# Attention on one core: score and value matmuls in runs of nine pairs instead of three, row sums off TensorE, one FFN unit per half

## Chip, cores, metric

One core of a Trainium2 chip runs the whole program. The metric is device time in microseconds (us) from one launch. The kernel before takes 952.02 us, the median of 3 runs (951.53 to 952.89).

## The reference

Two blocks follow each other, in float32. The first is attention over 8 batches, 8 heads, 1152 keys and head size 64. Its queries are the means of two neighbours, so there are 576 of them.

```python
q_pool = q.reshape(B, H, S // 2, 2, D).mean(axis=3)
scores = (1 / np.sqrt(D)) * np.matmul(q_pool, k.transpose(0, 1, 3, 2))
attn = np.exp(scores - scores.max(-1, keepdims=True))
attn = attn / (attn.sum(-1, keepdims=True) + 1e-09)
x = np.matmul(attn, v)            # then (B, H, S, D) -> (B, S, H*D): 576 rows of 512
```

The second, for each batch, takes the 128 rows of x with the highest gate score and adds an FFN's result to them; other rows pass through.

```python
scores = np.einsum('bsd,d->bs', x, w_gate)
top = np.argpartition(-scores[b], 128)[:128]
h = np.maximum(x[b, top] @ w1, 0.0)             # 512 -> 1024
out[b, top] = x[b, top] + sigmoid(scores[b, top])[:, None] * (h @ w2)
```

## The kernel before

Heads are worked in pairs, 32 pairs in all, four to a batch. A pair's keys lie in 9 chunks of 128, its 576 queries in two halves of 288. The scores of one chunk and one half are two matmuls, one per head, on the upper and the lower 64 rows of TensorE (L710): this is a *score pair*. It writes one PSUM buffer of two banks (pool `ps_sc`, three buffers). ScalarE takes the exponential of both heads in one instruction (L717), without a maximum. The *value pair* of the chunk is again two matmuls, one per head, on the left and the right 64 columns (L727); nine such pairs add up in one PSUM bank `av`. The profile shows each float32 matmul as two instructions, so a pair counts four.

The order of the work is written out in `run` and kept (`manual_schedule`): each engine does its instructions in the order in which they are written. The loop takes steps. A step is a group of three chunks (`G = 3`): three score pairs of this group, then three value pairs of the group before. Three steps are a half, six a pair of heads.

The row sums of the exponentials are made in two parts: `added` (L745, L755, L756) adds the nine chunks of a half on VectorE, and in `normalized` two matmuls with ones (L770) sum over the partitions, a step after the half's end. VectorE turns `av` into the layout of x by 32x32 transposes (`drained`, L760). There is only one `av` buffer, so the next half's first value matmul waits for that. `normalized` also transposes the sums (L778), adds 1e-9 (L780), takes the reciprocal (L784) and multiplies (L786), all on VectorE. Once a pair, `finished` writes x to a scratch tensor in DRAM (SyncE's queue, L798), multiplies by the gate weights on GpSimd (L803) and sums on VectorE (L809).

`load_pair` brings k, q and v of the next pair on SyncE's queue, two buffers each for k and q. `prepare_pair` adds neighbouring queries on GpSimd (L692) and transposes k and q on VectorE (L697, L698), in a pair's fourth step.

`routed` is a generator with the FFN block of one batch: one unit of it is issued in each step that does not normalise. Its parts are the gate's row sums (`line`, `diag`, L826, L830), their spread over all partitions by matmul (L842) and copy on ScalarE (L849), the scores as columns (L651), the gate's exponential on ScalarE (L858), the ranks by comparisons on VectorE (L880 to L910), the picks (L916), their matmul (L926), a gather (L938), the transposes of the picked rows (L953), the FFN's matmuls (L965 in two units, L977), and a scatter (L992). It uses the one PSUM buffer of `misc`. The last batch runs its generator after the loop. `outside` (L1009 to L1025) counts sums out of bounds, for a slower path that isn't taken here.

Of the kernel before, what the change touches and what calls it, by code (L numbers as in the profile page):

```python
# [13 lines left out]
G = 3  # L14
# [520 lines left out]
class _Plain:  # L535
# [10 lines left out]
    def __init__(self, ctx, tc, q, k, v, moe_w_gate, moe_w1, moe_w2, capacity, out):  # L546
# [43 lines left out]
        self.ps_ms = pool("ps_ms", 1, space=psum)  # L590
        self.constants()
# [8 lines left out]
    def constants(self):  # L600
# [29 lines left out]
        self.columns(self.token, line_f)  # L630
# [9 lines left out]
        self.sums = const.tile([P, self.B * self.NPAIR * 2, self.HB], F32, name="sums")  # L640
# [4 lines left out]
    def columns(self, to, line):  # L645

        nc, NF = self.nc, self.NF
        ps = self.misc()
# [19 lines left out]
    def load_pair(self, b, hp):  # L668
        nc = self.nc
        kb = self.load.tile([P, self.KB, BLK], F32, name="kb")  # L670
        qb = self.load.tile([P, self.QB, 2, BLK], F32, name="qb")
        v_sb = self.load.tile([P, 2, self.NC, self.D], F32, name="v_sb", bufs=3)
        for j, ds, rows in self.quarters():
            h = 2 * hp + j
            nc.sync.dma_start(  # L675
                kb[rows, :, :], self.k[b, h, :, ds].rearrange("(n i) d -> i n d", i=BLK)
            )
            nc.sync.dma_start(  # L678
                qb[rows, :, :, :].rearrange("i n r d -> i (n r) d"),
                self.q[b, h, :, ds].rearrange("(i m) d -> i m d", i=BLK),  # L680
            )
# [6 lines left out]
    def prepare_pair(self, pair):  # L688

        nc = self.nc  # L690
        qp = self.load.tile([P, self.QB, BLK], F32, name="qp", bufs=1)
        nc.gpsimd.tensor_tensor(  # L692
            out=qp[:, :, :], in0=pair["q"][:, :, 0, :], in1=pair["q"][:, :, 1, :], op=ALU.add
        )
        pair["kT"] = self.load.tile([P, self.S], F32, name="kT")
        pair["qT"] = self.load.tile([P, self.Sp], F32, name="qT")
        nc.vector.transpose(pair["kT"][:, :], pair["k"].rearrange("p n d -> p (n d)"))  # L697
        nc.vector.transpose(pair["qT"][:, :], qp.rearrange("p n d -> p (n d)"))  # L698

    def scores(self, grp):  # L700

        nc, pair, n = self.nc, grp["pair"], self.HALF
        qs = slice(grp["s"] * n, (grp["s"] + 1) * n)
        grp["p"] = self.work.tile([P, G, 2, n], F32, name="p", bufs=5)
        for u in range(G):
            c = grp["g"] * G + u
# [10 lines left out]
            nc.scalar.activation(grp["p"][:, u, :, :], sc[:, :, 0:n], AF.Exp, scale=self.scale)  # L717

    def weighted(self, grp):

        nc, n = self.nc, self.HALF
        if grp["g"] == 0:
# [425 lines left out]
```

## Time and profile before

| | us |
|---|---|
| median of 3 runs | 952.02 |
| the profiled execution | 951.33 |
| its span (first to last instruction) | 949.5 |
| TensorE matmuls busy | 844.1 (89%) |
| VectorE busy | 629.0 (66%) |
| ScalarE busy | 359.5 (38%) |
| GpSimd busy | 109.4 (12%) |
| mean granted clock of TensorE, of full | 0.946 |

The rest of the profiled execution's time lies around the span. Busy times overlap. A matmul's end is modelled, so a high share of TensorE does not by itself say that it runs at its best; what it does in a stretch is read from the starts of its runs. An instruction waits for a semaphore at the head of its engine's queue, and what is behind it waits too. [...]

### The profile page before, as it was taken

How to read it: one execution, taken by the hardware profiler on the slowest of the kernel's cores; microseconds unless marked ns; L12 is line 12 of the kernel's file. 1: busy time of each engine (PE TensorE's matmuls, PEld its weight loads, DVE VectorE, ACT ScalarE, POOL GpSimd, SP SyncE). 2: the span in 40 equal slices, each digit the busy share in tenths (PEclk: the TensorE clock that was granted, in tenths of full speed). 3: DMA queues.
4: the chain of work that ended last, by engine and by line, in shares of the span. 5: the costliest groups of instructions: out<-in, count | busy, mean ns of one | idle time of the engine just before them, and what ended most of it. 6: DMA issues, size and time to landing. Idle time of an engine off the chain costs nothing.

```text
span 949.5 us, 14253 instructions
## 1 busy us (share of the span) xinstructions
PE 844.1 (89%) x5695; PEld 500.2 (53%) x5695; DVE 629.0 (66%) x1069; ACT 359.5 (38%) x625; POOL 109.4 (12%) x91
## 2 busy tenths in 40 slices
PE   4999888998899988999879989799889998889736
PEld 2555545654456554565446545465455654556324
DVE  2888777566875678746787376865777567874540
ACT  2544443434343344325424344343443334433200
POOL 1111111011110111102011111011111011110100
PEclk9999998999999999999999999899998999989958
DMA  9987774766834676545767437557464667810120
GB/s 134 249 135 103 125 105 60 83 99 109 104 56 61 94 138 88 76 61 74 125 88 99 60 77 117 82 88 99 89 97 64 76 99 118 108 24 7 25 67 14
DMA packets 453419, 84.97 MB, mean 89 GB/s; under 512 B 450528, under 2 KB 450528, under 8 KB 453088
## 3 DMA queue, kind: packets, MB, share of 16 engines
q1 hardware_dynamic: 452064, 79.79, 57.5%
q0 software_dynamic: 1280, 4.20, 1.6%
q8 instruction: 46, 0.75, 0.4%
q14 instruction: 29, 0.24, 0.1%
HBM read 72.42 MB, written 20.97 MB: 98 GB/s over the span
## 4 chain that ended last, share of the span: by engine, by line
issue 39%; PE 27%; DVE 18%; SPq 5%; POOL 5%; DMA 4%; ACT 2%; POOLq 0%; DVEq 0%
PE sc L710 9%; PE av L727 8%; DVE acc L745 6%; PE ps L965 6%; DMA qb<-in_q_dram 3%; POOL qp L692 3%; SPq L675 2%; SPq L798 2%; DVE cmp L889 2%; PE ps L977 1%; SPq L678 1%; ACT p L717 1%; DVE sum L755 1%; POOL prod L803 1%; PE ps L926 1%
## 5 line engine op out<-in xcount | busy, mean ns | idle before, releaser
L717 ACT ACTIVATE p<-sc 128x576 f32<-128x576 f32 x576 | 336.1, 651 | 408.3 <-PE sc L710 389.6
L710 PE MATMUL sc<-qT,kT 64*128 64x288 f32 x2304 | 352.3, 438 | 9.9 <-DVE qT L698 9.9
L727 PE MATMUL av<-p,v_sb 128*64 128x288 f32 x2304 | 332.2, 425 | 22.7 <-DVE avb L760 22.7
L710 PEld LDWEIGHTS sc<-qT,kT 64*128 64x128 f32 x2304 | 221.0, 195 | 124.3 <-issue 71.8
L727 PEld LDWEIGHTS av<-p,v_sb 128*64 128x64 f32 x2304 | 152.3, 140 | 181.7 <-issue 77.1
L745 DVE TENSOR_TENSOR acc<-p 128x1728 f32<-128x1728 f32 x64 | 124.6, 1947 | 115.4 <-ACT p L717 115.1
L745 DVE TENSOR_TENSOR acc<-acc,p 128x1728 f32<-128x1728 f32 x64 | 137.0, 2141 | 10.0 <-ACT p L717 9.5
L803 POOL TENSOR_TENSOR prod<-x,w_gate 128x576 f32<-128x576 f32 x32 | 44.9, 1403 | 568.9 <-DVE x L786 568.9
L760 DVE STREAM_TRANSPOSE avb<-av 128x288 f32<-128x288 f32 x64 | 30.6, 478 | 60.0 <-PE av L727 60.0
L965 PE MATMUL ps<-xeT,w 128*128 128x128 f32 x512 | 63.4, 284 | 1.4 <-ACT hT L972 0.7
L965 PEld LDWEIGHTS ps<-xeT,w 128*128 128x128 f32 x512 | 60.3, 197 | 8.1 <-issue 5.3
L977 PE MATMUL ps<-w,hT 128*128 128x512 f32 x128 | 57.1, 599 | 0.7 <-ACT hT L972 0.7
L809 DVE TENSOR_REDUCE part<-prod 128x18 f32<-128x576 f32 x32 | 24.1, 753 | 48.7 <-POOL prod L803 48.7
L755 DVE TENSOR_TENSOR sum<-acc 128x576 f32<-128x576 f32 x64 | 49.6, 775 | 2.2
L756 DVE TENSOR_TENSOR sum<-sum,acc 128x576 f32<-128x576 f32 x64 | 49.6, 775 | 2.2
L692 POOL TENSOR_TENSOR qp<-qb 128x576 f32<-128x576 f32 x32 | 45.9, 1435 | 22.8 <-DMA qb<-in_q_dram 22.6
L697 DVE STREAM_TRANSPOSE kT<-kb 128x1152 f32<-128x1152 f32 x32 | 43.0, 1345 | 6.2 <-DMA kb<-in_k_dram 6.2
L770 PE MATMUL ps<-sum,ones 128*64 128x288 f32 x256 | 42.7, 413 | 1.5 <-DVE sum L756 1.5
L977 PEld LDWEIGHTS ps<-w,hT 128*128 128x128 f32 x128 | 23.7, 190 | 30.7 <-issue 29.8
L926 PE MATMUL ps<-meta,pick 128*128 128x3 f32 (+1 forms) x80 | 15.3, 310 | 27.3 <-DVE pick L916 27.3
L972 ACT ACTIVATE hT<-ps 128x512 f32<-128x512 f32 x16 | 9.6, 597 | 73.8 <-PE ps L965 73.8
L984 DVE SCALAR_TENSOR_TENSOR xe<-ps,own_gate,xe 128x512 f32<-128x512 f32 x8 | 6.0, 751 | 41.9 <-PE ps L977 41.9
(64 smaller groups left out, 307.6 us busy)
## 6 DMA issues: line engine op xcount, KB each, us to landing
kb<-in_k_dram SPq DMA_DIRECT2D x128, 144.0 KB, 4.6
qb<-in_q_dram SPq DMA_DIRECT2D x128, 144.0 KB, 4.8
v_sb<-in_v_dram SPq DMA_DIRECT2D x64, 288.0 KB, 5.3
xs<-x SPq DMA_DIRECT2D x128, 72.0 KB, 2.3
out_dram<-xs SPq DMA_DIRECT2D x8, 1152.0 KB, 5.7
w<-in_moe_w_dram SPq DMA_DIRECT2D x2, 2048.0 KB, 11.1
xe<-xs,index POOLq DMA_INDIRECT x8, 3.5
out_dram<-xe,index POOLq DMA_INDIRECT x8, 4.4
```

The costliest lines, as they stand in the source:

```text
L692: nc.gpsimd.tensor_tensor(out=qp[:, :, :], in0=pair["q"][:, :, 0, :], in1=pair["q"][:, :, 1, :], op=ALU.add)
L697: nc.vector.transpose(pair["kT"][:, :], pair["k"].rearrange("p n d -> p (n d)"))
L710: nc.tensor.matmul(sc[:, j, 0:n], lhsT=pair["kT"][rows, c * P : (c + 1) * P], rhs=pair["qT"][rows, qs], start=True, stop=True,)
L717: nc.scalar.activation(grp["p"][:, u, :, :], sc[:, :, 0:n], AF.Exp, scale=self.scale)
L727: nc.tensor.matmul(self.av[j * self.D : (j + 1) * self.D, 0:n], lhsT=grp["pair"]["v"][:, j, c, :], rhs=grp["p"][:, u, j, :], start=(c == 0 ...
L745: nc.vector.tensor_tensor(out=acc[:, :, :], in0=first[:, :, :], in1=grp["p"].rearrange("p u j n -> p u (j n)"), op=ALU.add,)
L755: nc.vector.tensor_tensor(out=to, in0=acc[:, 0, :], in1=acc[:, 1, :], op=ALU.add)
L756: nc.vector.tensor_tensor(out=to, in0=to, in1=acc[:, 2, :], op=ALU.add)
L770: nc.tensor.matmul(ps[j * self.D : (j + 1) * self.D, 0:n], lhsT=self.ones[:, 0 : self.D], rhs=half["sum"][:, j, :], start=True, stop=True,)
L803: nc.gpsimd.tensor_tensor(out=prod[:, :, :], in0=x[:, hp, :, :], in1=self.w_gate[:, hp : hp + 1, :].broadcast_to([P, self.QB, BLK]), op=AL ...
L965: nc.tensor.matmul(pv[:, f, 0:w], lhsT=self.w1[:, c, (f0 + f) * P : (f0 + f + 1) * P], rhs=xeT[:, c, 0:w], start=(c == 0), stop=(c == self ...
L977: nc.tensor.matmul(ps[0:w, 0 : self.Dm], lhsT=hT[:, f, 0:w], rhs=self.w2[:, f, :], start=(f == 0), stop=(f == self.NFC - 1),)
```

## The change

- `scores` and `weighted` work a whole half: nine score pairs of half h, then nine value pairs of half h - 1. The exponentials of a half are one tile.
- The row sums are made by `folded`: GpSimd adds chunks 0 to 2 and 3 to 5; VectorE sums that and chunks 6 to 8 with two reduces that transpose 32x32 blocks on the way (so they sum over 32 partitions), and a third small reduce. One matmul a pair with a 0/1 matrix (`merge`) sums over the four blocks of partitions and spreads the result.
- `normalized` works once a pair. The product of `avb` and the reciprocals moves from VectorE to GpSimd.
- FFN units are issued at one point of each half, after the value pairs (`between`), one unit of each active generator. Those with larger outputs take a buffer of `ps_sc`. L965 becomes one unit; the two row matmuls and their copies become one.
- k and q get one buffer instead of two. The first pair is loaded and prepared in two parts, its q by ScalarE's queue. The weights' loads come one half later; a pair is prepared at the start of the half before it is used.
- After the loop the comparisons are not divided into units, and `outside` runs behind the gather.

```diff
+        self.merge = const.tile([P, P // BLK, BLK], F32, name="merge")
+        nc.vector.tensor_copy(
+            self.merge[:, :, :], self.same[:, :].unsqueeze(1).broadcast_to([P, P // BLK, BLK])
+        )
...
-    def load_pair(self, b, hp):
+    def load_pair(self, b, hp, parts=1):
-        kb = self.load.tile([P, self.KB, BLK], F32, name="kb")
-        qb = self.load.tile([P, self.QB, 2, BLK], F32, name="qb")
+        kb = self.load.tile([P, self.KB, BLK], F32, name="kb", bufs=1)
+        qb = self.load.tile([P, self.QB, 2, BLK], F32, name="qb", bufs=1)
+        nk, nq = self.KB // parts, self.QB // parts
+        other = nc.sync if parts == 1 else nc.scalar
...
-    def scores(self, grp):
+    def scores(self, half):
-        grp["p"] = self.work.tile([P, G, 2, n], F32, name="p", bufs=5)
-        for u in range(G):
-            c = grp["g"] * G + u
+        p = half["p"] = self.work.tile([P, self.NG, G, 2, n], F32, name="p")
+        for c in range(self.NC):
             sc = self.ps_sc.tile([P, 2, 512], F32, name="sc")
...
-            nc.scalar.activation(grp["p"][:, u, :, :], sc[:, :, 0:n], AF.Exp, scale=self.scale)
+            nc.scalar.activation(p[:, c // G, c % G, :, :], sc[:, :, 0:n], AF.Exp, scale=self.scale)
...
+    def folded(self, half):
+        nc, nb, p, pair = self.nc, 2 * self.HB, half["p"], half["pair"]
+        acc = self.work.tile([P, G * 2 * self.HALF], F32, name="acc")
+        groups = p.rearrange("p g u j n -> p g (u j n)")
+        nc.gpsimd.tensor_tensor(
+            out=acc[:, :], in0=groups[:, 0, :], in1=groups[:, 1, :], op=ALU.add
+        )
+        fold = self.small.tile([P, 2, G * nb], F32, name="fold")
+        for a, of in enumerate((groups[:, 2, :], acc[:, :])):
+            nc.vector.tensor_reduce(
+                fold[:, a, :],
+                of.rearrange("p (m d) -> p m d", d=BLK),
+                AX.X,
+                ALU.add,
+                apply_transpose=True,
+            )
+        if half["s"] == 0:
+            pair["sum"] = self.small.tile([P, 2, nb], F32, name="sum")
+        nc.vector.tensor_reduce(
+            pair["sum"][:, half["s"], :],
+            fold.rearrange("p a (u n) -> p n (a u)", n=nb),
+            AX.X,
+            ALU.add,
+        )
...
+    def normalized(self, pair, ps):
+        nc, hb, hp, x = self.nc, self.HB, pair["hp"], pair["x"]
+        nc.tensor.matmul(
+            ps[:, 0 : 4 * hb],
+            lhsT=self.merge.rearrange("p g j -> p (g j)"),
+            rhs=pair["sum"].rearrange("p s n -> p (s n)"),
+            start=True,
+            stop=True,
+        )
...
+        rec = self.small.tile([P, self.QB], F32, name="rec")
         nc.vector.reciprocal(rec[:, :], tot)
-        x = half["x"]
-        nc.vector.tensor_tensor(
-            out=x[:, pair["hp"], s * hb : (s + 1) * hb, :],
-            in0=half["avb"][:, :, :],
-            in1=rec[:, :].unsqueeze(2).broadcast_to([P, hb, BLK]),
+        nc.gpsimd.tensor_tensor(
+            out=x[:, hp, :, :],
+            in0=pair["avb"][:, :, :],
+            in1=rec[:, :].unsqueeze(2).broadcast_to([P, self.QB, BLK]),
             op=ALU.mult,
         )
...
+    def wide(self):
+        return self.ps_sc.tile([P, 2, 512], F32, name="sc")
...
+    def between(self, pair):
+        ps = self.misc()
+        if pair:
+            self.normalized(pair, ps)
+        for unit in list(self.routing):
+            try:
+                unit.send(ps)
+            except StopIteration:
+                self.routing.remove(unit)
+        if pair and pair["hp"] == self.NPAIR - 1:
+            unit = self.routed(pair["b"], pair["xs"], pair["part"])
+            next(unit)
+            self.routing.append(unit)
...
+        upcoming = self.load_pair(*pairs[0], parts=2)
+        self.prepare_pair(upcoming, parts=2)
+        for h in range(n_halves + 1):
+            if h < n_halves:
...
+                    if following:
+                        upcoming = self.load_pair(*following)
+                elif following:
+                    self.prepare_pair(upcoming)
+                if h == 1:
+                    self.load_weights()
+                half = {"pair": pair, "s": s}
+                halves.append(half)
+                self.scores(half)
+                self.folded(half)
+            if h > 0:
+                done = halves[h - 1]
+                self.weighted(done)
+                self.drained(done)
+                self.between(done["pair"] if done["s"] == 1 else None)
```

In the changed `routed` the units end (`yield`) after: line and diag; the row matmuls and copy; the columns, the gate's exponential and the comparisons of row tiles 0 and 1; those of 2 and 3; tile 4, rank and picks; the picks' matmul and gather; the transposes; L965; L977 and scatter.

## Rows read from the trace of the kernel before

**Rows 1.** The page's first part: busy us (share of the span) of each engine.

```profile
PE 844.1 (89%) x5695; PEld 500.2 (53%) x5695; DVE 629.0 (66%) x1069; ACT 359.5 (38%) x625; POOL 109.4 (12%) x91
```

**Rows 2.** Chain of waits, in order of time: start us, length us, what.

```profile
678.04 24.05 issue
...
791.27 24.05 issue
```

**Rows 3.** Timeline of TensorE, normal steps: start us, us, what; x12 are three pairs.

```profile
697.77 1.68 PE L727 MATMUL av<-p,v_sb 128*64 128x288 f32 x12
699.28 0.66 PE L770 MATMUL ps<-sum,ones 128*64 128x288 f32 x4
699.86 1.73 PE L710 MATMUL sc<-qT,kT 64*128 64x288 f32 x12
701.52 1.68 PE L727 MATMUL av<-p,v_sb 128*64 128x288 f32 x12
703.12 1.73 PE L710 MATMUL sc<-qT,kT 64*128 64x288 f32 x12
```

**Rows 4.** Timeline of TensorE, the three waits: in brackets the idle time, its releaser.

```profile
682.48 0.75 PE L842 MATMUL ps<-diag,ones 128*128 128x288 f32 x2 [2.81 <-DVE diag L830]
...
711.03 3.13 PE L727 MATMUL av<-p,v_sb 128*64 128x288 f32 x12 [2.92 <-DVE avb L760]
...
723.46 1.48 PE L926 MATMUL ps<-meta,pick 128*128 128x3 f32 x9 [2.29 <-DVE pick L916]
```

**Rows 5.** Stretch after the second wait: us, busy us, granted clock, DMA, GB/s.

```profile
711.00:714.60 3.60, 3.57 (x18) 1.68 (x18) 3.60 (x14) 0.00 (x0) 0.00 (x0) 0.58 1.57 133
```

**Rows 6.** Timeline of TensorE, two FFN units of the same batch.

```profile
736.56 0.66 PE L953 MATMUL ps<-ident,xe 128*128 128x128 f32 x4
...
761.96 7.13 PE L977 MATMUL ps<-w,hT 128*128 128x512 f32 x16
```

**Rows 7.** Timeline of ScalarE: exponentials, four of the start and three of a step.

```profile
17.66 2.32 ACT L717 ACTIVATE p<-sc 128x576 f32<-128x576 f32 x4 [0.31 <-PE sc L710]
...
700.73 1.74 ACT L717 ACTIVATE p<-sc 128x576 f32<-128x576 f32 x3 [2.01 <-PE sc L710]
```

**Rows 8.** Groups by line: busy us, mean ns, then idle us before and releasers.

```profile
L717 ACT ACTIVATE p<-sc 128x576 f32<-128x576 f32 x576 | 336.1, 651 | 408.3 <-PE sc L710 389.6 <-DVE sums L780 14.7 <-DVE smb L778 2.4
...
L697 DVE STREAM_TRANSPOSE kT<-kb 128x1152 f32<-128x1152 f32 x32 | 43.0, 1345 | 6.2 <-DMA kb<-in_k_dram 6.2
...
L809 DVE TENSOR_REDUCE part<-prod 128x18 f32<-128x576 f32 x32 | 24.1, 753 | 48.7 <-POOL prod L803 48.7
...
L698 DVE STREAM_TRANSPOSE qT<-qp 128x576 f32<-128x576 f32 x32 | 23.6, 737 | 1.2 <-POOL qp L692 1.2
L889 DVE TENSOR_SCALAR_CACHE_REDUCE cmp<-sc_row,gate_sc 128x576 f32<-128x576 f32 (+4 forms) x40 | 21.6, 540 | 0.3
```

**Rows 9.** Timeline of GpSimd and VectorE, side by side, at two places.

```profile
24.10 2.40 POOL L692 TENSOR_TENSOR qp<-qb 128x576 f32<-128x576 f32 x1 [10.61 <-DMA qb<-in_q_dram]
...
25.27 1.85 DVE L755 TENSOR_TENSOR sum<-acc 128x576 f32<-128x576 f32 x1
...
703.49 1.40 POOL L692 TENSOR_TENSOR qp<-qb 128x576 f32<-128x576 f32 x1
703.56 0.75 DVE L809 TENSOR_REDUCE part<-prod 128x18 f32<-128x576 f32 x1 [1.52 <-POOL prod L803]
```

**Rows 10.** Waits: engine line, for what, us in total, times, longest us.

```profile
ACT gate L858 <- DVE gate L855: 13.2, 8, 1.7
```

**Rows 11.** Timeline of the start: GpSimd waits for the third pair's q.

```profile
48.08 1.47 POOL L692 TENSOR_TENSOR qp<-qb 128x576 f32<-128x576 f32 x1 [3.24 <-DMA qb<-in_q_dram]
```

**Rows 12.** Timeline of TensorE, the end: last values, row matmul, L965's second unit.

```profile
892.54 3.13 PE L727 MATMUL av<-p,v_sb 128*64 128x288 f32 x24
...
905.01 1.33 PE L842 MATMUL ps<-diag,ones 128*128 128x288 f32 x2 [1.56 <-DVE gate_sc L654]
...
931.40 3.84 PE L965 MATMUL ps<-xeT,w 128*128 128x128 f32 x32 [0.69 <-ACT hT L972]
```

More of the change, by code (lines that the diff above doesn't have):

```diff
@@ L808, in finished @@
         )
-        nc.vector.tensor_reduce(half["part"][:, hp, :], prod[:, :, :], AX.X, ALU.add)
+        nc.vector.tensor_reduce(pair["part"][:, hp, :], prod[:, :, :], AX.X, ALU.add)
     def misc(self):
         return self.ps_ms.tile([P, 512], F32, name="ps")
+    def wide(self):
+        return self.ps_sc.tile([P, 2, 512], F32, name="sc")
     def routed(self, b, xs, part):
@@ L907, in routed @@
             )
-            if t % 2 == 1:
+            if t % 2 == 1 and not self.ending:
                 yield
+        nc.vector.tensor_scalar(
+            out=gate[:, :], in0=gate[:, :], scalar1=1.0, scalar2=None, op0=ALU.add
+        )
+        meta = ffn.tile([P, NT, 3], F32, name="meta")
+        nc.vector.tensor_copy(meta[:, :, 0], self.token[:, :])
+        nc.vector.tensor_scalar(
+            out=meta[:, :, 1], in0=self.token[:, :], scalar1=float(b * Sp), scalar2=None, op0=ALU.add
+        )
+        nc.vector.reciprocal(meta[:, :, 2], gate[:, :])
         nc.vector.tensor_reduce(rank[:, :], parts[:, :, :], AX.X, ALU.add)
@@ L1063, in run @@
-                self.scores(groups[step])
-            if 1 <= step <= n_groups:
-                self.weighted(groups[step - 1])
-            if step < n_groups:
-                self.added(groups[step], halves[step // self.NG])
-            if step >= 1 and step % self.NG == 0:
-                self.drained(halves[step // self.NG - 1])
-            if step >= self.NG + 1 and step % self.NG == 1:
-                half = halves[step // self.NG - 1]
-                self.normalized(half)
-                if half["s"] == 1:
-                    self.finished(half)
-                    if half["pair"]["hp"] == self.NPAIR - 1:
-                        for _ in routing:
-                            pass
-                        routing = self.routed(half["pair"]["b"], half["xs"], half["part"])
-            else:
-                next(routing, None)
@@ L1081, in run @@
-            if step < n_groups and i == 3 and n + 1 < len(pairs):
-                self.prepare_pair(upcoming)
-        count = self.outside()
-        for _ in routing:
-            pass
-        return nc.values_load(count[0:1, 0:1])
+                    pair.update(x=x, xs=xs, part=part)
+                    if following:
[4 more added lines that the diff above has]
+                    self.load_weights()
```

216 lines of the change are left out of this document (93 added, 123 removed).

## Prediction, made before the changed kernel was run

> **What bounds the kernel now.** I read the engine totals first: TensorE is busy for 844 of 949.5 us, VectorE for 629, ScalarE for 360, GpSimd for 109 [rows 1]. TensorE works through its queue in order and sets the end. The chain of waits then shows a batch in steady state: two like points of it lie 113.2 us apart [rows 2]. The rest comes from the timeline inside one batch.
>
> A step (three score pairs, three value pairs) starts its scores at 699.86, its values at 701.52, the next scores at 703.12: 1.66 + 1.60 us. The column-sum matmuls are one more pair in the values' form, and with them the stretch 697.77 to 699.86 is 2.09, so one pair costs 2.09 - 1.60 = 0.49 [rows 3]. Three pairs are 1.46; the 0.20 and 0.14 over that are paid where scores turn into values and back: 0.34 a step. A half is 3 x 3.26 + 0.49 = 10.27 us, eight of them 82.2. That leaves 31 of 113.2 for FFN matmuls and waits. Of waits the timeline shows three, 2.81 for diag, 2.92 for avb, 2.29 for pick, all VectorE's. [...] With 3.13 - 1.68 = 1.45 each, the three cost 4.3 + 4.4 + 3.7 = 12.4 a batch, and some 18 are FFN matmuls.
>
> **The change, for one batch.**
>
> *Switches.* Two of three steps' switches go in each half: 2 x 0.34 x 8 = -5.5.
>
> *Sums.* The sum pair goes, 0.49 x 8 = -3.9. The new merge matmul (one a pair of heads, two passes) lies between nothing and the 0.66 of L953's four passes [rows 6]; I take 0.3, x 4 = +1.2. The score rows' two matmuls are joined and L965 is in one piece: two or three switches fewer, -0.4.
>
> *ScalarE's pace.* Scores now run nine pairs on three PSUM buffers, so pair nine waits for the sixth exponential. The first exponential starts 0.87 after the first pair (699.86 to 700.73). Three take 1.74, four 2.32, one 0.65 [rows 3, 7, 8]: they start 0.55 apart. The sixth ends at 0.87 + 5 x 0.55 + 0.65 = 4.27. TensorE alone would be there after 8 x 0.485 + 0.10 = 3.98 (0.10 for a run's first pass, my estimate from its 1.73 busy over 1.66). With 0.05 for the signal pair nine starts at 4.32, and a restarted pair pays the 0.10 again: 0.44 x 8 = +3.5. A half is now 5.1 + 4.5 = 9.6. Without the wait this is 0; with the whole run at ScalarE's pace it is 1.0 x 8 = 8.
>
> *The three waits.* VectorE loses its adds and a transpose, and gets two transposing reduces of 1728 elements a half, which this trace doesn't have. By the transposes (0.74 for 576, 1.345 for 1152: 1.05 ns an element over 0.13 [rows 8]) one is 1.95, and not under 1.8, those elements without the 0.13; if it went over its data twice, the second time like L809 (0.753 for 576 [rows 8]), it were 1.95 + 2.26 = 4.2. I take 1.95: a transpose and a reduce of 576 take 0.74 and 0.75, so neither is slow, and a pass that does both is nearest to them. GpSimd's add of 1728 elements is three times qp's 1.40 [rows 9], 4.2; not under VectorE's 1.95, at most three times the blocked 2.40 [rows 9], 7.2.
>
> [...]
>
> In a half, counted from its first score: exponentials done at 5.9, GpSimd's add from 4.3 to 8.5, the second reduce ends at 10.5, the fold at 10.8, avb of the half before at 11.3. The next values need avb at 9.6 + 5.1 = 14.7, so 3.4 are to spare. Diag and pick are read a whole half later. All three waits hide: -12.4.
>
> *A new wait.* The exponential of the gate (L858) stands in ScalarE's queue ahead of the next half's exponentials, and waits for VectorE. It falls into a half in which a pair is normalised. There VectorE goes on after avb at 11.3: totals and reciprocal to 11.9; GpSimd's x and prod, 1.4 each, to 14.7; the part reduce 0.75; gate copies and clamp 0.5: 16.0, and the exponential ends at 16.25. TensorE begins the next half at 9.6 + 0.3 + 0.4 = 10.3, and its first exponential could start at 11.15. It is 5.1 late, and TensorE stands after three pairs. Before, this wait was 13.2 us over eight, 1.7 at most [rows 10], since the queue before it was short. A wait of this length leaves TensorE at the low clock: 1.45 more. +6.6 a batch. Covered it would cost 0; with the next half's reduces and avb sliding behind it, 9.
>
> *kT.* VectorE transposes kT and qT at the start of a pair's second half, behind any late unit; 0.8 a batch for the one with picks (0 to 2).
>
> Sum: -5.5 - 3.9 + 1.2 - 0.4 + 3.5 - 12.4 + 6.6 + 0.8 = -10.1, so 103.1 a batch. Seven batches carry routing: -70.7.
>
> **Ends.** Start: the loads in two parts let scores begin some 5 us sooner, but nothing comes of it: pair three's q lands at 48.08 [rows 11], behind two pairs and the weights, and the same bytes are ahead of it in the new order, with one buffer instead of two. At that point a half's values are still owed (4.5) where now a step's are (1.6): +2.9. The batch without routing saves 2.3 in its second half by the terms above and 1.7 of small avb waits: -1.1 in all. End: the seventh batch's L977 (7.1 [rows 6]) now comes after the last values, beside the normalising of the last half: -7.1 before that point. After it VectorE and GpSimd need 0.9 for avb, 0.6, 1.45 for x, 1.4 for prod, 0.8, which L977's 7.4 outlasts; then xe, line and diag: 9.5. It is 905.01 - 895.67 = 9.3 now [rows 12]. Then one row copy less, -0.6, and L965 without its gap of 0.69 [rows 12]: -1.1 in all.
>
> 949.5 - 70.7 - 1.1 - 7.1 - 1.1 = 869.5 for the span. The profiled execution took 951.33, 1.83 over its span, and lies 0.7 below the median: 872 for the median. About 0.2% is what a measurement of this kernel can tell from no change.
>
> **Rivals.**
>
> *1, faster: the gate's exponential holds nobody up,* because the order in ScalarE's queue isn't the written one: -6.6 x 7, 826. For it: nothing but that the order isn't in the trace. Against: 16 us of listed work and 11.15 to do it in. 0.06.
>
> *2: a reduce costs 2.5 to 3.4.* VectorE's average still fits, but in the three halves with rank work avb comes late: at 3.0 each, 2.1 later, less what is to spare behind the unit, some 5 us a batch with the low clock: 872 + 35 = 907. For it: the form isn't in the trace. 0.14.
>
> *3, slower: VectorE becomes the bound.* Its place is its queue, through avb, which each half's values wait for. With r for one reduce, a pair of heads asks of it 4r + 0.6 fold + 1.0 avb + 2.1 kT, qT + 0.6 + 2.8 waiting for GpSimd + 0.75 = 4r + 7.85, and a batch's routing some 10 (an estimate: L889 is 21.6 in eight batches, 2.7 each [rows 8], and the other compares, ties, picks and copies are put at two to three times that), with 7 of waiting for L977: 16r + 48.4. At r = 4.2 that is 115.6: 12.5 x 7 a batch over, and 5.3 x 4 in the first, less the gate wait that is then counted twice, 6.6: 872 + 102 = 974. It binds from r = 3.4 and makes the kernel slower from r = 4.05. For it: a reduce that must transpose first. Against: transposes and reduces alone take the same time. 0.08.
>
> *4: GpSimd locks VectorE out.* qp at 24.10 takes 2.40 for 1.40, and the sum at 25.27 takes 1.85 for the 0.76 of others, until qp ends; yet the part reduce at 703.56 runs its 0.75 beside qp's 1.40 [rows 9]. So adds of two inputs don't run together on the two engines, and a reduce does run beside GpSimd's. In the change GpSimd's add holds 4.2 in each half; VectorE's own with two inputs are diag and five tie operations. Blocked once by 4.2 in each of three halves with nothing to spare, 12.6, less 6 that the gate wait covers: +6.6 x 7 = 918. I expect near 0: the ties stand ahead of a reduce that waits for the same add. 0.06.
>
> [...]
>
> *5: within 0.2%,* two of these together: 0.02.
>
> **Numbers.** Likeliest 872, chance 0.64; its own range is 848 (no pacing by ScalarE, gate wait 5) to 894 (pacing 5, adds of 5). With rivals 2 and 4 some 0.8 lie within 842 to 918; rivals 1 and 3 and some ends are left out. Faster 0.90, same 0.02, slower 0.08.
>
> **What would show it.** Value runs of nine pairs in 4.4 us; a score run of about 5.0 with exponentials 0.55 apart; no TensorE wait of over 1 us for diag, avb or pick; one wait of some 5 us a batch in a score run, where ScalarE stands on the gate, with a low clock behind it; reduces of 1.95, GpSimd's add of 4.2; batches 103 apart; last values at about 817. The prediction is wrong if the reduces exceed 3, or if avb releases the value runs.

## The result, and the profile after

The changed kernel takes 877.83 us, the median of 4 runs (876.72 to 878.25), against 952.0 for the kernel before on the same chip: a ratio of 0.9218, 95% interval [0.9202, 0.9234]. The forecast was 872.0, its range 842 to 918. The profiled execution took 876.72, its span is 874.9 (before 949.5), the mean granted clock 0.962 (0.946).

The page's first part for the changed kernel, where [rows 1] stood:

```profile
PE 786.5 (90%) x5503; PEld 478.2 (55%) x5503; DVE 504.4 (58%) x848; ACT 345.0 (39%) x617; POOL 396.1 (45%) x188
```

VectorE lost 125 us of work and GpSimd gained 287. TensorE is still the busiest engine. The groups by line and shape say what one of each new instruction costs (busy us, mean ns, then idle us before it):

```profile
L762 POOL TENSOR_TENSOR acc<-p 128x1728 f32<-128x1728 f32 x64 | 247.3, 3865 | 209.2 <-ACT p L740 208.2
...
L767 DVE TRANSPOSE_TENSOR_REDUCE fold<-acc 128x54 f32<-128x1728 f32 x64 | 126.1, 1971 | 27.2 <-POOL acc L762 27.2
L767 DVE TRANSPOSE_TENSOR_REDUCE fold<-p 128x54 f32<-128x1728 f32 x64 | 125.8, 1965 | 167.2 <-ACT p L740 167.2
...
L916 DVE SCALAR_TENSOR_TENSOR tie<-sc_row,gate_sc,before 64x64 f32<-64x64 f32 x8 | 26.0, 3256 | 0.0
...
L916 DVE SCALAR_TENSOR_TENSOR tie<-sc_row,gate_sc,before 128x128 f32<-128x128 f32 x32 | 11.1, 347 | 0.0
```

The reduce costs what was predicted (1.97 for 1.95), the add on GpSimd somewhat less (3.87 for 4.2). The last two rows don't fit: the tie operation (it counts equal scores for the rank, once for each of a batch's five row tiles) of the fifth tile has a quarter of the others' elements and takes nine times as long. We come back to it.

Now TensorE's waits (engine line, for what: us in total, times, longest), and the one of ScalarE that was forecast ([rows 10] before):

```profile
PE sc L733 <- ACT p L740: 20.6, 7, 3.1
PE sc L733 <- DVE qT L719: 20.2, 10, 5.0
PE ps L953 <- DVE pick L943: 12.8, 8, 7.0
PE ps L656 <- DVE sums L806: 9.4, 7, 1.3
PE sc L992 <- ACT hT L1000: 5.5, 8, 0.7
```

```profile
ACT gate L887 <- DVE rank_parts L890: 69.2, 8, 9.7
```

The three waits of [rows 4] are gone for avb and diag; for pick 0.8 a batch is left. The forecast wait is there, seven times. The waits for sums and for hT were not forecast, and the one for qT is longer than forecast. The timeline of one batch shows two plain runs, the wait ahead of the columns (L656), and the score run in which ScalarE stands on the gate's exponential (in brackets the idle time and its releaser):

```profile
321.32 5.03 PE L733 MATMUL sc<-qT,kT 64*128 64x288 f32 x36
...
326.28 4.59 PE L748 MATMUL av<-p,v_sb 128*64 128x288 f32 x36
...
332.55 0.44 PE L656 MATMUL ps<-ident,sc_row 1*128 1x1 f32 x5 [1.34 <-DVE sums L806]
...
332.92 2.15 PE L733 MATMUL sc<-qT,kT 64*128 64x288 f32 x12
...
336.91 0.21 ACT L887 ACTIVATE gate<-gate 128x5 f32<-128x5 f32 x1 [9.74 <-DVE rank_parts L890]
...
337.71 4.76 PE L733 MATMUL sc<-qT,kT 64*128 64x288 f32 x24 [2.64 <-ACT p L740]
...
342.39 2.89 PE L748 MATMUL av<-p,v_sb 128*64 128x288 f32 x22
```

A plain score run lasts 326.28 - 321.32 = 4.96, the one with the gate 342.39 - 332.92 = 9.47, and in the stretch from 333.0 to 342.4 the granted clock is 0.64 of full. Two halves later:

```profile
361.16 0.75 DVE L834 TENSOR_REDUCE part<-prod 128x18 f32<-128x576 f32 x1 [2.75 <-POOL prod L828]
...
362.47 3.83 POOL L762 TENSOR_TENSOR acc<-p 128x1728 f32<-128x1728 f32 x1
...
362.50 0.27 DVE L906 TENSOR_SCALAR_CACHE_REDUCE cmp<-sc_row,gate_sc 64x64 f32<-64x64 f32 x1
...
362.70 3.69 DVE L916 SCALAR_TENSOR_TENSOR tie<-sc_row,gate_sc,before 64x64 f32<-64x64 f32 x1
...
367.13 1.36 PE L953 MATMUL ps<-meta,pick 128*128 128x3 f32 x10 [0.83 <-DVE pick L943]
...
369.94 5.01 PE L733 MATMUL sc<-qT,kT 64*128 64x288 f32 x36 [1.45 <-DVE qT L719]
...
371.59 1.93 DVE L767 TRANSPOSE_TENSOR_REDUCE fold<-acc 128x54 f32<-128x1728 f32 x1
...
375.81 3.87 POOL L762 TENSOR_TENSOR acc<-p 128x1728 f32<-128x1728 f32 x1
375.81 1.98 DVE L767 TRANSPOSE_TENSOR_REDUCE fold<-p 128x54 f32<-128x1728 f32 x1 [1.30 <-ACT p L740]
```

GpSimd begins the add at 362.47. The tie behind it on VectorE, 0.27 of work in the kernel before, ends at 366.39, the add at 366.30, and the picks and qT with it are late. A compare beside the same add (362.50, 0.27) and a transposing reduce beside the next one (375.81, 1.98) take their usual time (0.27 and 1.97 on the mean of their groups).

**Where the time went.** Row matmuls mark the batches; the first and the seventh, in the kernel before and in the changed one:

```profile
114.74 0.75 PE L842 MATMUL ps<-diag,ones 128*128 128x288 f32 x2 [2.81 <-DVE diag L830]
...
795.70 1.14 PE L842 MATMUL ps<-diag,ones 128*128 128x288 f32 x2 [2.81 <-DVE diag L830]
```

```profile
110.25 1.24 PE L870 MATMUL sc<-diag,ones 128*128 128x288 f32 x4
...
741.61 1.24 PE L870 MATMUL sc<-diag,ones 128*128 128x288 f32 x4
```

There were 113.5 a batch between them, there are 105.2. Six such batches give -49.6 (forecast 6 x -10.1 = -60.6). From the seventh to the end of the last values (895.67 before [rows 12], 824.0 now) it is 82.4 instead of 100.0, -17.6; up to the first, -4.5. These marks lie differently in the two orders of work, so the two stretches are taken in sum: -22.1 (forecast -1.1 for the start, -10.1 - 7.1 for the other, -18.3). The tail behind the last values went from 53.8 to 50.9, -2.9 (forecast -1.1). Sum -74.6, as the spans say.

### The profile page after: what moved, and what is told of

Read it like the earlier page. It is cut to its first block, busy times and chain, and to the rows that moved or that the text cites. A ratio compares the mean times of both kernels' runs of the same rounds, so it can differ in the third digit from the quotient of the medians.

```text
span 874.9 us, 13669 instructions
## 1 busy us (share of the span) xinstructions
PE 786.5 (90%) x5503; PEld 478.2 (55%) x5503; DVE 504.4 (58%) x848; ACT 345.0 (39%) x617; POOL 396.1 (45%) x188
## 4 chain that ended last, share of the span: by engine, by line
PE 58%; DVE 14%; POOL 11%; ACT 7%; DMA 4%; issue 3%; SPq 2%; ACTq 0%; POOLq 0%; DVEq 0%
PE sc L733 24%; PE av L748 20%; PE sc L992 7%; POOL acc L762 7%; ACT p L740 6%; PE sc L1007 6%; DVE fold L767 3%; DVE tie L916 3%; POOL prod L828 2%; DMA qb<-in_q_dram 2%; POOL x L815 2%; DMA xe<-xs,index 2%; DVE part L834 1%; DVE kT L715 1%; SPq L685 1%
## 5 line engine op out<-in xcount | busy, mean ns | idle before, releaser
L733 PE MATMUL sc<-qT,kT 64*128 64x288 f32 x2304 | 340.6, 448 | 40.8 <-ACT p L740 20.6
L762 POOL TENSOR_TENSOR acc<-p 128x1728 f32<-128x1728 f32 x64 | 247.3, 3865 | 209.2 <-ACT p L740 208.2
L748 PE MATMUL av<-p,v_sb 128*64 128x288 f32 x2304 | 293.5, 409 | 0.7 <-DVE avb L787 0.7
L767 DVE TRANSPOSE_TENSOR_REDUCE fold<-p 128x54 f32<-128x1728 f32 x64 | 125.8, 1965 | 167.2 <-ACT p L740 167.2
L767 DVE TRANSPOSE_TENSOR_REDUCE fold<-acc 128x54 f32<-128x1728 f32 x64 | 126.1, 1971 | 27.2 <-POOL acc L762 27.2
L992 PE MATMUL sc<-xeT,w 128*128 128x128 f32 x512 | 64.1, 286 | 6.2 <-ACT hT L1000 5.5
L992 PEld LDWEIGHTS sc<-xeT,w 128*128 128x128 f32 x512 | 61.1, 199 | 11.2 <-ACT hT L1000 7.0
L1007 PE MATMUL sc<-w,hT 128*128 128x512 f32 x128 | 56.8, 597 | 0.0
L712 POOL TENSOR_TENSOR qp<-qb 128x576 f32<-128x576 f32 (+1 forms) x33 | 45.1, 1368 | 21.1 <-DMA qb<-in_q_dram 21.0
L715 DVE STREAM_TRANSPOSE kT<-kb 128x1152 f32<-128x1152 f32 (+1 forms) x33 | 44.0, 1333 | 14.1 <-DMA kb<-in_k_dram 14.1
L965 POOL DMA_INDIRECT xe<-xs,index x8 | 8.5, 1067 | 70.3 <-DVE own_gate L963 58.9
L787 DVE STREAM_TRANSPOSE avb<-av 128x288 f32<-128x288 f32 x64 | 30.4, 476 | 11.9 <-PE av L748 11.3
L916 DVE SCALAR_TENSOR_TENSOR tie<-sc_row,gate_sc,before 128x128 f32<-128x128 f32 (+1 forms) x40 | 37.1, 928 | 0.0
```

Source lines behind the costliest of these rows:

```text
L712: nc.gpsimd.tensor_tensor(out=qp[:, qs, :], in0=pair["q"][:, qs, 0, :], in1=pair["q"][:, qs, 1, :], op=ALU.add)
L715: nc.vector.transpose(pair["kT"][:, i * nk * BLK : (i + 1) * nk * BLK], pair["k"][:, ks, :].rearrange("p n d -> p (n d)"),)
L733: nc.tensor.matmul(sc[:, j, 0:n], lhsT=pair["kT"][rows, c * P : (c + 1) * P], rhs=pair["qT"][rows, qs], start=True, stop=True,)
L748: nc.tensor.matmul(half["av"][j * self.D : (j + 1) * self.D, 0:n], lhsT=half["pair"]["v"][:, j, c, :], rhs=half["p"][:, c // G, c % G, j, ...
L762: nc.gpsimd.tensor_tensor(out=acc[:, :], in0=groups[:, 0, :], in1=groups[:, 1, :], op=ALU.add)
L767: nc.vector.tensor_reduce(fold[:, a, :], of.rearrange("p (m d) -> p m d", d=BLK), AX.X, ALU.add, apply_transpose=True,)
```

## The experiments

The theory at this point was that of the forecast with one term added: the gate's wait is the largest loss left, some 4.4 a batch; the rival, that VectorE and GpSimd set the pace between columns and picks and that the gate's wait covers it. The experiments ran in three groups on three chips; the kernel before took 951.87 to 952.53 there (medians), so their times are compared as they stand.

**1 and 2. The gate's exponential one unit later; the ties ahead of the other comparisons, and the fifth tile's comparisons one unit earlier.**

```diff
         for t, rows in tiles:
+            if t == 2:
+                nc.scalar.activation(gate[:, :], gate[:, :], AF.Exp, scale=-1.0)
```

> The changed kernel (877.8 us) with the gate's exponential issued one unit later, so that in ScalarE's queue it stands behind the next half's exponentials and finds its input ready. Nothing else moves. Theory (ScalarE held up in order by an exponential that waits for VectorE): in seven batches the score run behind it, 9.5 us and 8.2, falls to 4.96; with 4.70 in most batches and 3.2 in two that is some 30 us: 845 to 850. Rival (VectorE is late at that place whatever the order, and another of its results will be waited for there): the wait moves to the merge or column matmuls, and the time stays above 868.

It took 885.85 (884.92 to 887.01), 0.9298 [0.9273, 0.9324]: the gate's wait is gone and the kernel is 8 us slower than the change. That is the rival's side, but what is waited for are picks and qT, not merge or columns. Timeline of GpSimd and VectorE at three places of one batch:

```profile
234.86 3.85 POOL L762 TENSOR_TENSOR acc<-p 128x1728 f32<-128x1728 f32 x1 [0.33 <-ACT p L740]
235.36 3.50 DVE L917 SCALAR_TENSOR_TENSOR tie<-sc_row,gate_sc,before 128x128 f32<-128x128 f32 x1
...
247.19 3.23 DVE L917 SCALAR_TENSOR_TENSOR tie<-sc_row,gate_sc,before 128x128 f32<-128x128 f32 x1
...
260.92 3.66 DVE L917 SCALAR_TENSOR_TENSOR tie<-sc_row,gate_sc,before 64x64 f32<-64x64 f32 x1
```

TensorE's waits name what is late then (12.8 in the change):

```profile
PE ps L954 <- DVE pick L944: 32.8, 8, 7.0
```

With the exponentials on time GpSimd's adds are on time too, and three ties a batch last 3.2 to 3.7 beside them instead of one. The late exponential had kept two of them apart.

```diff
             own = sc[0:rows, t : t + 1]
+            tie = ffn.tile([P, P], F32, name="tie")
+            nc.vector.scalar_tensor_tensor(
...
-            if t % 2 == 1 and not self.ending:
+            if t == 1 and not self.ending:
                 yield
+        if not self.ending:
+            yield
```

> The changed kernel with the comparisons of the fifth row tile issued one unit earlier, and each tie operation ahead of the other comparisons of its tile; the gate's exponential is left where it was. Theory (GpSimd's add of 3.86 us shuts out the fifth tile's tie, 3.69 us for 0.27, and with it picks, kT and qT): the tie falls to 0.3, TensorE's waits for pick (0.83) and qT (1.45) vanish with what they cost in low clock, 0 to 2.5 after them: 2.3 to 4 in seven batches, 16 to 28 us, so 850 to 862. Rival (VectorE is simply full in that half, the tie's 3.4 us would be waited for elsewhere): within 5 us of 877.8.

875.48 (873.58 to 878.07), 0.9196 [0.9165, 0.9227], the rival's result. The ties are free; now a plain VectorE operation of 5 elements a partition is where the add falls:

```profile
363.18 3.84 POOL L762 TENSOR_TENSOR acc<-p 128x1728 f32<-128x1728 f32 x1
363.24 3.81 DVE L935 TENSOR_SCALAR meta<-token 128x5 f32<-128x5 f32 x1
```

So moving one instruction doesn't help here: another, 0.15 in the change, falls beside the add and takes 3.81.

**3 and 4. No add on GpSimd: three reduces a half on VectorE; then the late exponential with it.**

```diff
-        nc.gpsimd.tensor_tensor(
-            out=acc[:, :], in0=groups[:, 0, :], in1=groups[:, 1, :], op=ALU.add
-        )
-        fold = self.small.tile([P, 2, G * nb], F32, name="fold")
-        for a, of in enumerate((groups[:, 2, :], acc[:, :])):
+        fold = self.small.tile([P, self.NG, G * nb], F32, name="fold")
+        for a in range(self.NG):
```

> The changed kernel (877.8 us) with the row sums of all nine chunks by transposing reduces on VectorE, three a half instead of two, and no add on GpSimd. The gate's exponential stays where it was. Theory (in e1 the ties were shut out by GpSimd's add, 3.2 to 3.7 us each, and so VectorE held up picks, kT and qT; the add is what has to go): no tie above 0.4 us; TensorE's waits for pick (0.83) and qT (1.45) go with the slow score run behind them (0.8 in the mean), and the gate's exponential comes 0.8 sooner since no reduce waits for the add: about 4 us in seven batches, 28, so 846 to 856. Rival (VectorE's work, 1.97 us more a half, holds up the values through avb): waits for avb appear and the time is 870 or more.

851.17 (848.54 to 855.72), 0.8939 [0.8909, 0.8969], as expected. The groups by shape have the tie back at its own price, and the wait for picks is gone in the loop, although VectorE does one reduce more a half:

```profile
L763 DVE TRANSPOSE_TENSOR_REDUCE fold<-p 128x54 f32<-128x1728 f32 x192 | 362.8, 1940 | 58.3 <-ACT p L740 58.3
...
L912 DVE SCALAR_TENSOR_TENSOR tie<-sc_row,gate_sc,before 64x64 f32<-64x64 f32 x8 | 2.2, 273 | 0.0
```

The add was worth -26.7, net of that reduce. Some 22 of it is what picks, qT and the slow score run behind them cost in the change, 0.83 + 1.45 + 0.92 on the mean in seven batches; the wait ahead of the columns is shorter as well (3.4 us in all for 9.4), which would fit that no reduce waits for the add any more. With the exponential of experiment 1 on top:

> As e5_three_reduces, and the gate's exponential one unit later, as in e1. Theory: without the add the 3.9 us that the wait for the gate costs beyond e5 come back this time, 27 us in seven batches, 818 to 828, where in e1 the same edit lost 8. Rival (the stretch from gate to picks is bound by VectorE with or without the add): within 8 us of e5.

846.74 (843.75 to 847.35), 0.8892 [0.8863, 0.8921]: the rival. The gate's wait is gone, yet only 4.4 us come back of some 35 (in experiment 3's profiled execution the seven score runs with the gate are 5.0 longer on the mean than a plain one). VectorE's timeline between the columns and the picks shows why:

```profile
353.54 0.75 DVE L830 TENSOR_REDUCE part<-prod 128x18 f32<-128x576 f32 x1 [2.75 <-POOL prod L824]
...
355.75 1.06 DVE L940 TENSOR_SCALAR pick<-slot_f,rank 128x128 f32<-128x128 f32 x5
356.74 1.36 DVE L715 STREAM_TRANSPOSE kT<-kb 128x1152 f32<-128x1152 f32 x1
...
358.69 5.65 DVE L763 TRANSPOSE_TENSOR_REDUCE fold<-p 128x54 f32<-128x1728 f32 x3
...
364.84 0.48 DVE L783 STREAM_TRANSPOSE avb<-av 128x288 f32<-128x288 f32 x1
```

Its one pause is the 2.75 for GpSimd's product, ahead of the part sum; picks, kT, qT, reduces and avb follow without a gap, and TensorE waits for several of them: 1.45 a batch for qT, 0.2 for picks, and now and then for avb.

**5 and 6. Runs of three again**, once in experiment 1's kernel, once in experiment 4's, there with the reduces spread over the half and avb ahead of the last.

```diff
+            for g in range(self.NG):
+                if h < n_halves:
+                    self.scores(half, g)
+                if h > 0:
+                    self.weighted(halves[h - 1], g)
```

> As e1_gate_late, but with three score and three value pairs in turn, as in the kernel before; sums, units and their places stay those of the change. Theory (nine pairs save 0.34 for each of two switches a half and give 0.39 back to ScalarE's pace): a half goes from 4.96 + 4.52 = 9.48 to 3 x 3.26 = 9.78, +0.30 in 64 halves, 19 us over e1; avb is now needed some 1.7 us after a half's start instead of 5.0 and may add up to 10. So 864 to 876. Rival (the long runs are worth all their switches, ScalarE's pace costs nothing): 0.68 x 64 = 44 us, 889. Rival 2 (run length is worth nothing, the gain was all in the waits): as e1.

994.08 (991.39 to 995.69), 1.0442 [1.0414, 1.0469]; the theory and both rivals missed. TensorE waits for avb 36 times:

```profile
PE av L751 <- DVE avb L790: 64.8, 36, 3.3
```

In runs of three the exponentials end only with the half, so the reduces end late, and avb stands behind them in VectorE's queue while the next values are due one step later, not one score run of nine. That speaks for the queue and not for the size of a run, so the second kernel mends the order:

> As e6, with three score and three value pairs in turn. Unlike e3 each reduce stands behind the scores it needs, and avb's transpose ahead of the last reduce, so that avb comes about 1 us into the next half, where it is needed at 1.7. Theory: what is left between e7 and e6 is the switches less ScalarE's pace, 9.78 for 9.48 a half, 19 us in 64 halves: 837 to 850. Rival (nine pairs are worth both switches whole): 44 us over e6. Rival 2 (the long run's worth is only that avb has time): avb waits of TensorE return here too, and e7 is 60 us or more over e6.

891.54 (888.88 to 895.8), 0.937 [0.9344, 0.9396], 44.8 above experiment 4. That is the first rival's number, but not its mechanism. Halves without any wait last 3 x 3.26 = 9.78 against 4.91 + 4.52 = 9.43 there: 0.35 x 64 = 22 of the 44.8 are the switches, less ScalarE's pacing. TensorE's waits for avb (27.5, 14 times, after 3.3) and for sums ahead of the columns (19.9, 7 times, after 3.4) hold most of the rest; the one for qT is shorter (8.6 after 20.6). So here runs of nine are worth about as much by the slack that they give VectorE as by the switches.

**7. Half of each exponential** in experiment 1's kernel (the other half of each chunk's queries is left out, and the probabilities there are a constant, in two fixed tiles).

```diff
-            nc.scalar.activation(p[:, c // G, c % G, :, :], sc[:, :, 0:n], AF.Exp, scale=self.scale)
+            nc.scalar.activation(
+                p[:, c // G, c % G, :, 0 : n // 2], sc[:, :, 0 : n // 2], AF.Exp, scale=self.scale
+            )
```

> As e1_gate_late, with exponentials of the first 144 columns of each head's half only; the other columns of two fixed tiles hold ones, so half of the scores are left out. TensorE's work is the same. Theory (ScalarE's exponentials, 0.55 apart, hold up pairs seven to nine of a run through the three PSUM buffers): score runs fall from 4.96 to 4.57, -0.39 in 64 halves, 25 us under e1, about 820 to 825. Rival (the 4.96 is TensorE's own, weights and first passes): score runs stay at 4.96 and the time within 4 us of e1.

873.47 (870.53 to 874.71), 0.916 [0.9131, 0.9189]. A plain score run is 4.57 instead of 4.96, so ScalarE's pace costs 0.39 a half (forecast 0.44), 3.1 a batch. Row matmuls lie 104.3 apart after 106.3: 2.1 of the 3.1 arrive. So the theory's place and size are right and the rival is out, but the time falls by 12.4 and not by 25. Of what is missing, 0.6 a batch are longer waits for qT (18.0 instead of 14.4 us over six batches); the score runs behind such waits are slower too (behind the picks 2.2 over a plain run on the mean, 1.5 in experiment 1; mean granted clock of the profiled executions 0.948, there 0.950). And the first row matmul comes 3.1 later, as the constant is written ahead of it.

**8. The kernel before, with diag and pick read one step later.** This takes two of the three waits out and nothing else.

```diff
         yield
+        yield
         sc_row = ffn.tile([P, Sp], F32, name="sc_row")
...
             yield
+            yield
             ps = self.misc()
```

> The kernel before (952 us) with one more step between diag and the matmul that reads it, and between the picks and theirs; nothing else. Theory (two of the three waits of a batch are there because TensorE reads what VectorE has just been given; read a step later they hide): 4.3 for diag and 3.7 for pick in seven batches, 56 us: 893 to 900, with the avb wait left. Rival (VectorE is behind in these steps anyway, and avb takes over): above 930.

902.53 (901.87 to 904.08), 0.9492 [0.9466, 0.9519]: -49.3, just short of the theory: 7.0 a batch, where the forecast had 4.3 + 3.7 = 8.0 for these two waits and the slow run behind each (1.45, the run behind avb in [rows 4] over that of [rows 3]): in the kernel before 3.16 behind diag, at a granted clock of 0.51 (683.2 to 686.6), and 3.00 behind the picks, at 0.50 (725.0 to 727.0), where another takes 1.73. Two thirds of what the whole change gains can be had without it. TensorE's waits show the third of them, for avb, still there, and a new one, for exponentials behind that of the gate:

```profile
PE av L727 <- DVE avb L760: 18.7, 16, 1.7
PE sc L710 <- ACT p L717: 18.5, 7, 2.6
```

**9 and 10. Two buffers, each alone.** L992 in two score buffers of four chunks; the columns (L656) in a score buffer instead of the one that the sums are read from.

```diff
-            for f0 in range(0, self.NFC, 8):
-                pv = self.wide().rearrange("p b (c n) -> p (b c) n", n=P)
-                nf = min(8, self.NFC - f0)
+            for f0 in range(0, self.NFC, 4):
+                pv = self.wide()[:, 0, :].rearrange("p (c n) -> p c n", n=P)
+                nf = 4
```

> The change, with the first FFN matmuls (L992) in two score buffers of four chunks each instead of eight chunks in one buffer. Theory: the 0.96 us in the middle of that run is the fifth chunk waiting until ScalarE has read the first four out of the same buffer; with a buffer of its own it goes, and the run takes about 7.3 instead of 8.29 us, eight times: about 8 us less, 868 to 871. Rival, the step as the prediction had it (one piece costs no more than two, a switch less): within 2 us of the change, 876 to 880.

876.6 (875.59 to 878.61), 0.9226 [0.9192, 0.9259], which is the time of the change: the rival's number, though not for its reason. The gap did go: L992 takes 7.34 instead of 8.29 in each of the seven batches. The 0.95 came back in the score run behind the picks. It lasts 4.95 in the first batch and 7.28 to 7.48 in six, 7.07 on the mean; in the change 4.95 in three and 6.3 to 7.5 in four, mean 5.88. Windows over picks and that run (us, busy us, granted clock, DMA, GB/s), first the change, then this kernel:

```profile
367.00:370.00 3.00, 1.43 (x12) 1.35 (x12) 3.00 (x8) 0.00 (x0) 0.00 (x0) 1.00 0.00 0
370.00:374.90 4.90, 4.90 (x38) 2.95 (x38) 4.45 (x6) 4.12 (x8) 0.18 (x1) 1.00 0.85 133
```

```profile
366.00:369.00 3.00, 1.43 (x12) 1.36 (x12) 3.00 (x8) 0.00 (x0) 0.00 (x0) 0.80 0.00 0
369.00:376.40 7.40, 7.40 (x38) 5.46 (x40) 4.43 (x6) 4.71 (x8) 1.77 (x2) 0.62 0.78 126
```

The run starts behind the same wait for qT, 1.45 in both, and does the same work, once at full clock and once at 0.62. The mean granted clock is lower in all six runs of this kernel (0.944 to 0.956) than in the four of the change (0.958 to 0.962). Why the clock falls more often after this wait here than in the change stays open.

```diff
-        self.columns(sc, sc_row, at_ps[:, 64 : 64 + NT])
+        self.columns(sc, sc_row, self.wide()[:, 0, 0:NT])
```

> The change, with the columns of the scores (L656) in a score buffer instead of the buffer that the sums are read from. The wait of about 1.3 us ahead of them goes either way. Theory: the gate's exponential later in the same batch waits for VectorE's and GpSimd's work, not for these matmuls, so its wait grows by what this one loses, and the time stays: 875 to 879. Rival: the gate's wait stays as it is and the 1.3 us are gained seven times: 867 to 870.

883.38 (879.38 to 888.06), 0.9287 [0.9247, 0.9327], some 5 us slower than the change. The wait of 1.3 ahead of the columns is gone, and the score run behind has grown from 9.2 on the mean of seven to 11.3 (in an execution of 888.06, the slowest of the six). Its timeline names a new releaser:

```profile
342.94 6.57 PE L733 MATMUL sc<-qT,kT 64*128 64x288 f32 x28 [3.95 <-DVE gate_sc L661]
```

The columns hold one of three score buffers until VectorE has copied them, and that copy stands behind the part sum. The run stands after two pairs instead of three, is released 5.20 after its start instead of 4.79, and then has seven pairs instead of six to do, 6.49 after 4.68, at a granted clock of 0.70 on the mean of the run (338.0 to 349.4; in the change 0.64 from 333.0 to 342.4). Both forecasts missed. The theory (the next wait takes it all) was right in that nothing is gained, but it overlooked that the columns then hold what the scores need.

**11 and 12. Together.** Experiment 4 with both edits of buffers, and then with the units issued ahead of the part sum, so that VectorE has work in the 2.75:

> Three reduces a half on VectorE, no add on GpSimd, the gate's exponential one unit later, and the two edits of buffers (columns in a buffer of their own, L992 in two pieces) together. Theory: with three reduces and the later exponential alone it was 846.7; L992 gives 1.0 us eight times, and the wait ahead of the columns, 0.56 there, comes off in part: 834 to 840. Rival: VectorE sets the pace of the stretch between them and gives it back: over 843.

838.96 (837.2 to 840.16), 0.883 [0.8798, 0.8862], as expected. The columns' buffer is waited for here as well, 1.46 a batch ([1.46 <-DVE gate_sc L661] in the score run at 326.74).

```diff
-            self.normalized(pair, ps)
+            prod = self.normalized(pair, ps)
         for unit in list(self.routing):
...
+        if pair:
+            self.nc.vector.tensor_reduce(
+                pair["part"][:, pair["hp"], :], prod[:, :, :], AX.X, ALU.add
+            )
```

> As the kernel with the four edits, and the routing's unit is issued ahead of the gate's product sum of the pair, so that VectorE works on comparisons and picks in the 2.75 us in which it otherwise stands for GpSimd's product. Theory: where a batch's picks, and the transposes of the next keys and queries behind them, were waited for (2.1 and 1.45 us, with a slow score run behind), VectorE is now 2.5 us earlier; 3 to 4 us a batch go, seven times: 21 to 28 less than that kernel, 808 to 819. Rival: the time is that of the reduces behind, which wait for the exponentials anyway, and the waits move to the next unit: within 6 us of that kernel.

826.4 (824.34 to 828.85), 0.8697 [0.8665, 0.873]: the fastest kernel here, 51 us below the change; -12.6 lies between theory and rival. It came at another place than the theory had: the score run behind the columns went from 6.99 to 4.91 in six batches and from 7.06 to 5.33 in one (14.2 in sum), as the copy no longer stands behind the part sum. Picks and what follows gained nothing, for this reason:

```profile
344.60 1.44 POOL L824 TENSOR_TENSOR prod<-x,w_gate 128x576 f32<-128x576 f32 x1
...
344.68 1.38 DVE L930 TENSOR_SCALAR meta<-token 128x5 f32<-128x5 f32 x1
...
346.00 1.41 POOL L712 TENSOR_TENSOR qp<-qb 128x576 f32<-128x576 f32 x1
...
346.23 2.03 DVE L940 TENSOR_SCALAR pick<-slot_f,rank 128x128 f32<-128x128 f32 x5
```

The operations that were moved into the wait for GpSimd now run beside GpSimd, and these two take longer there: 1.38 for 0.16 and 2.03 for 1.06 in experiment 4.

## Why the prediction was near, and which steps failed

The forecast was 5.8 us low on 878, and its direction and main terms held. But it is near partly by luck: steps erred in both directions, and the ends gave back half of what the batches cost too much. For a batch (mean of the first six), in us:

| step | predicted | measured | from |
|---|---|---|---|
| score run, value run | 5.1, 4.5 | 4.96, 4.52 | timeline |
| ScalarE's pace in it, a half | 0.44 | 0.39 | experiment 7 |
| merge matmul, each | 0.3 | 0.34 | timeline |
| transposing reduce; GpSimd's add | 1.95; 4.2 | 1.97; 3.87 | groups |
| waits for diag and avb | gone | gone | waits |
| diag's and pick's waits and the low clock behind (granted 0.51, 0.50) | 8.0 | 7.0, net of a new wait | experiment 8 |
| gate's wait with the low clock (granted 0.64) | 6.6 | 4.4 | timeline |
| columns wait for the sums | 0 | 1.3 | waits |
| picks late | 0 | 0.8 | waits |
| kT, qT and the low clock behind (granted 1.00 in three of the six, 0.61 to 0.76 in three) | 0.8 | 1.45 + 0.86 | timeline |
| L965 in one piece, row matmuls joined | -0.4 | +0.55 | timeline, experiment 9 |
| wait for the gathered rows | 0 | 0.4 | timeline |

The differences sum to about +2.0 with the shorter halves (8 x -0.12) and merges counted and without experiment 8's row, which is of another kernel; the marks give 105.2 - (113.5 - 10.1) = +1.8. Six times that is the +11.0 above. The other stretches gave 5.6 more than forecast: 3.4 up to the first mark and 0.4 behind the seventh, which I haven't split further, and 1.8 in the tail. There the way from the first row matmul to the columns fell from 3.63 to 1.97, where the forecast had -0.6 for one row copy less; the gap in L965 that it took out (-0.7) is still there, 0.69. No run takes the row sums (-3.9) or the wait for avb (-4.4) alone; that they are gone is read from the timeline and the waits.

**The step that failed most: rival 4.** "I expect near 0: the ties stand ahead of a reduce that waits for the same add." They do: the add is that of the next half, it starts at 362.47, as soon as GpSimd is through with qp, and VectorE, which has stood 2.75 for GpSimd's product, is then still at its comparisons. But between the ties and that reduce stand the picks, kT, qT and the reduce of the other chunks, none of which needs the add. The tie is held until 366.39; picks and qT come late and TensorE waits for them; and the reduce, at 371.59, finds the add long done. It happened in all seven batches that are routed in the loop, to one tie in each and not in three halves, as rival 4 had it. Its list of what can be locked out was too short as well: diag and the ties, but the plain one-input operations for meta and picks are held up too (3.81 for 0.15 in experiment 2, 2.03 for 1.06 in experiment 12). And the sum of [rows 9] does not end with qp: it ends 0.62 behind it (27.12 after 26.50), which fits that it is held until qp ends and then does its own work. Experiment 3 puts the whole add at 26.7 us, VectorE's extra reduce already paid, where rival 4 had 46 and the forecast nothing. What an add holds up is shown operation by operation: the tie (3.69 for 0.27) and the plain tensor_scalar of experiment 2 (3.81 for 0.15) last to its end, the compare at 362.50, a tensor_scalar that also sums, takes its 0.27, and the reduce at 375.81 its 1.98.

**The gate's wait is there, smaller and not a term of its own.** Its place and cause were as forecast, and so was the low clock (0.64 from 333.0 to 342.4). 4.4 instead of 6.6 mostly since 1.3 of the wait was already spent ahead of the columns; the shorter halves and the quicker add may be the rest, which isn't shown. But a sum of waits treats it as removable, and experiments 1 and 4 show that it isn't: without it the same stretch waits elsewhere, so that the kernel is 8.0 slower with GpSimd's add and only 4.4 faster without it. In that stretch the order of VectorE's own queue (experiment 12) took more out.

**The joined L965** was priced by its switches alone. The switches did give the 0.4: without its gap L992 takes 7.34 where the two units took 7.54, and the row matmuls take 1.17 after 1.37. But in one buffer of eight chunks the fifth waits for ScalarE's reading of the first four, 0.95. The columns' wait is of the same kind: sums and columns share a buffer, and the merge matmul of the change put a VectorE read of it just ahead.

**Held:** rivals 2 and 3 fell with the reduce's 1.97; rival 1 with the 69.2 that ScalarE stands on the gate; rival 5 with the interval. The move of the last FFN unit behind the last values came as forecast:

```profile
824.22 7.11 PE L1007 MATMUL sc<-w,hT 128*128 128x512 f32 x16
...
833.15 1.24 PE L870 MATMUL sc<-diag,ones 128*128 128x288 f32 x4 [1.81 <-DVE gate_sc L659]
```

Row matmuls 9.2 behind the last values (end 823.98), forecast 9.5, before 9.3 [rows 12]. The last values themselves end 7 later than the 817 forecast: the batches' +11.0 less what the start gave.

## What to carry to other kernels

When work moves to GpSimd, list the VectorE instructions that can run beside it for its whole length, those of the next iteration too, and see in a trace how long each takes there. Here a tie with two inputs (3.69 for 0.27) and a plain tensor_scalar (3.81 for 0.15) lasted as long as the add, a compare that also sums (0.27) and a transposing reduce (1.98) did not, and two reduces and an add lost to three reduces by 27 us. A wait found in a timeline is worth its length only if the engine that ends it has time to spare behind it; otherwise look at the order of that engine's queue, which gave 12.6 us without an instruction less. Before a matmul group is joined or gets another buffer, find who reads that buffer next and what that reader stands behind.

## What the runs showed of the hardware that was not expected

- A transposing reduce of 128x1728 float32 takes 1.93 to 1.98 us, some 1.13 ns an element, also beside GpSimd's add (1.98). That is what a transpose alone would take (1.95, an estimate from the transposes of 576 and 1152 elements, 0.74 and 1.345).
- Beside GpSimd's two-input add (3.83 and 3.84 us there) even small VectorE operations lasted to its end: 3.69 for 0.27 (two inputs; ended 366.39, the add 366.30), 3.81 for 0.15 (one input, 5 elements a partition; 367.05, the add 367.02).
- After the same wait of 1.45 us for qT the following run took 4.95 us in three batches of the change (granted clock 1.00) and 6.3 to 7.5 in four (0.61 to 0.76); in experiment 9 it was slow in six of seven (0.62 where it was read), and that undid a gain of 0.95 a batch made elsewhere.
